# Re-timing the loads and the attention ticks of a fused attention and mixture-of-experts kernel

## The chip, the cores and the metric

The kernel runs on one core of a Trainium2 chip. The metric is the time of one execution on the device, in microseconds (us). The engines are named as in the profile: PE (matrix multiply), DVE (vector), ACT (scalar), POOL and SP; SP and POOL also issue DMA transfers, each from a queue of its own that works in order.

## The reference

Eight sequences of 576 positions pass through a linear attention with 8 heads of 64, and then each whole sequence through one of 8 experts:

```python
# per batch b and head h, for q, k, v of shape (8, 8, 576, 64)
q_s = softmax(q, axis=-1)            # over the 64 channels
k_s = softmax(k, axis=2)             # over the 576 positions
attn = q_s @ (k_s.T @ v)             # (576, 64); heads side by side give x[b]: (576, 512)
# per sequence
logits = x[b].mean(axis=0) @ w_gate  # 8 experts
e = argmax(logits); g = softmax(logits)[e]
out[b] = g * (relu(x[b] @ w1[e]) @ w2[e])   # w1[e]: (512, 1024), w2[e]: (1024, 512)
```

Which expert a sequence takes is known only when its attention is done. With the inputs drawn here the eight sequences take the experts 2, 3, 3, 1, 3, 3, 4, 6: sequences 0, 1, 3, 6 and 7 need an expert that no earlier one had, and sequences 2, 4 and 5 take the one that sequence 1 brought in. All arithmetic of the matrix products is in 16 bit; inputs and weights are 32 bit in memory.

## The kernel before

**Tiles.** A sequence is loaded in two halves, numbered n = 2b and 2b+1, of four heads each. One `load(n)` (L114) is three transfers of 576 KB on SP's queue, q, k and v, each into one of three buffers, so load n+3 waits until n has been read. Per half, `exp_q` and `exp_k` are one ACT instruction each, `cast_v` is one on POOL (or ACT), `scale_q` (L140) is a sum and a reciprocal on DVE and one product, from half 4 on, on POOL. `kv_step` (L156) is 18 small matmuls on PE and four small DVE instructions; `t_step` (L174) transposes 9 blocks on PE into the same two banks of PSUM, and DVE copies them out; `x_step` (L187) multiplies, and DVE (L199) copies the result to `xt` with its row sums.

**Gate.** `gate_step` (L204) multiplies the row sums by `w_gate` on PE, finds the expert on DVE, loads its number into a POOL register and lets POOL issue the transfers of `w1` (L255) and `w2` (L266), 4.2 MB of 32-bit weights, which are cast to 16 bit on the way. There are five slots for weights. Sequence b always uses slot b % 5; if an earlier sequence already holds the expert, the transfers are issued under a condition that is false. `fetch` (L297) then copies each quarter of the weights on DVE from the slot that holds the expert to the sequence's own slot (from the slot to itself when the weights are new). A copy so waits for the transfers.

**Experts.** `moe(b)` (L311) is a generator of 17 units of PE work: 8 of the first product (L320, L325, evicted by ACT in L329), 8 halves of the second (L339), each second one followed by an eviction on ACT (L346) and two output transfers on SP (L348), and the last 64 positions (L354, L359, L361).

**The order of the work** is written out by hand: every engine works its instructions off in the order in which Python emits them. The steps of attention stand in a table of ticks (`at`, L371). A first stretch (L418 to L453) emits sequences 0 and 1; then a loop (L454) takes one unit of `moe(b)` after another, and after each it moves a clock `tick` forward and emits all steps that are due (`run_ticks`). Sequence b's attention stands at ticks 12b to 12b+10, its gate at 12b+10, and its `fetch` at 12(b+1)+6 to +9. In the emission order that follows, sequence 2's attention stands among the units of `moe(0)`, its gate after the first unit of `moe(1)`; sequence 3's attention stands in `moe(1)`, its gate after the first unit of `moe(2)`; and so on. `hold_loads` (L268) puts a tiny transfer on SP that reads from what the fourth of sequence 0's eight transfers of `w1` brings; load 4 and those after it stand behind it on SP's queue.

The lines quoted are those of the kernel before. The whole of it:

Of the kernel before, what the change touches and what calls it, by code (L numbers as in the profile page):

```python
# [10 lines left out]
FP16 = mybir.dt.float16  # L11
# [8 lines left out]
def kernel(  # L20
# [15 lines left out]
    nc = tc.nc  # L36

    B, H, S, Dh = q.shape
# [6 lines left out]
    ND = D // 128  # L45
# [3 lines left out]
    consts = ctx.enter_context(tc.tile_pool(name="consts", bufs=1))  # L49
# [27 lines left out]
    nc.vector.memset(ones_row, 1.0)  # L77
    hist = consts.tile([1, 8], FP32)
    nc.vector.memset(hist, -1.0)
    held = consts.tile([1, 8], FP16)  # L80
    own = consts.tile([1, NS, 8], FP32)
    nc.vector.memset(own, 0.0)
    for n in range(NS):
# [30 lines left out]
    def load(n, names="qkv"):  # L114
        if n >= 2 * B:
            return
        b, i = divmod(n, 2)
        for name in names:
            x = in_pool.tile([128, 2, J * Dh], FP32, name=f"{name}_in")
            nc.sync.dma_start(out=x, in_=pair_src({"q": q, "k": k, "v": v}[name], b, i))  # L120
            ins[n, name] = x.rearrange("p n (j d) -> p n j d", j=J)

    def exp_q(n):
        eq = e_pool.tile([128, J, 2, Dh], FP16, name="eq")
        nc.scalar.activation(out=eq.rearrange("p j n d -> p n j d"), in_=ins.pop((n, "q")), func=AF.Exp)  # L125
        halves[n] = {"eq": eq, "qt": {}, "kv": {}}

    def cast_v(n, on_act=False):
        dst = v_aug[n % NVB][:, :, 1:].rearrange("p j (n d) -> p n j d", n=2)
        if on_act:  # L130
            nc.scalar.copy(dst, ins.pop((n, "v")))
        else:
            nc.gpsimd.tensor_copy(out=dst, in_=ins.pop((n, "v")))  # L133
# [22 lines left out]
    def kv_step(n):  # L156
        ek, va, kps = halves[n]["ek"], v_aug[n % NVB], kv_banks(n)
        for j in range(J):
            for g in range(2):
                r = slice(64 * g, 64 * g + 64)  # L160
                nc.tensor.matmul(  # L161
                    kps[g][:, 0:129], lhsT=ek[r, j], rhs=va[r, j],
                    start=(j == 0), stop=(j == J - 1),
                )
        for g in range(2):
            icv = kv_pool.tile([128, 1], FP32, name="icv")
            nc.vector.reciprocal(out=icv, in_=kps[g][:, 0:1])
            kv = kv_pool.tile([128, 128], FP16, name="kv")
            nc.vector.scalar_tensor_tensor(
                out=kv, in0=kps[g][:, 1:129], scalar=icv, in1=blkmask, op0=ALU.mult, op1=ALU.mult,  # L170
            )
            halves[n]["kv"][g] = kv

    def t_step(n, g):  # L174
        eq = halves[n]["eq"]
        r = slice(64 * g, 64 * g + 64)
        tp = kv_banks(n)[g].bitcast(FP16)[:, 448:448 + S]
        for j in range(J):
            nc.tensor.transpose(out=tp[:, 64 * j:64 * j + 64], in_=eq[r, j], identity=ident[r, r])  # L179
        qt = qt_pool.tile([128, S], FP16, name="qt")  # L180
        if n < 2:
            nc.scalar.copy(qt, tp)
        else:
            nc.vector.tensor_copy(out=qt, in_=tp)  # L184
        halves[n]["qt"][g] = qt

    def x_step(n, g):  # L187
        b, i = divmod(n, 2)
        c = 2 * i + g
        if c == 0:  # L190
            xt = xt_pool.tile([128, ND, S], FP16, name="xt")
            pooled = gat_pool.tile([128, ND], FP32, name="pooled")
            seqs[b] = {"xt": xt, "pooled": pooled}
        xt, pooled = seqs[b]["xt"], seqs[b]["pooled"]
        kvs, qts = halves[n]["kv"], halves[n]["qt"]
        px = bank("x")
        nc.tensor.matmul(px[:, 0:SM], lhsT=kvs[g], rhs=qts[g][:, 0:SM], start=True, stop=True)  # L197
        nc.tensor.matmul(px[:, SM:S], lhsT=kvs[g], rhs=qts[g][:, SM:S], start=True, stop=True)  # L198
        nc.vector.tensor_tensor_reduce(  # L199
            out=xt[:, c, :], in0=px[:, 0:S], in1=ones_f32.to_broadcast([128, S]),  # L200
            scale=1.0, scalar=0.0, op0=ALU.mult, op1=ALU.add, accum_out=pooled[:, c:c + 1],
        )
# [62 lines left out]
            cs = slice(4 * hf, 4 * hf + 4)  # L265
            nc.gpsimd.dma_start(out=w2_all[:, b % NS, cs], in_=w2_src[:, cs], **seqs[b]["kw"])  # L266

    def hold_loads():  # L268

        nc.sync.dma_start(out=held, in_=w1_all[64:65, 0, ND - 1, 0:8])  # L270

    def gate_exp(b):
        ex = gat_pool.tile([1, E], FP32, name="ex")
# [91 lines left out]

    NA = 12
    ticks = {}

    def at(t, fn, *args):  # L371
        ticks.setdefault(t, []).append((fn, args))

    for b in range(B):
        for i in range(2 if b else 0):
            n, t0 = 2 * b + i, NA * b + 5 * i
            at(t0, kv_step, n)
            for g in range(2):
                at(t0 + 1 + g, t_step, n, g)
                at(t0 + 3 + g, x_step, n, g)  # L380
        at(NA * b + 10, gate_step, b)
        late = 0 if b else 5
        at(NA * b + 11 + late, gate_exp, b)
        at(NA * b + 12 + late, gate_split, b)
        at(NA * b + 14 + late, gate_spread, b)
        if b:
            for part in range(2):
                at(NA * (b + 1) + 6 + part, fetch, b, w1_all, part)
                at(NA * (b + 1) + 8 + part, fetch, b, w2_all, part)
    at(15, load_w2, 0)  # L390
    for n in range(4, 2 * B):
        t0 = NA * (n // 2) + 5 * (n % 2)
        x = 3 if n == 4 else 0
        at(t0 - 6 + x, exp_q, n)
        at(t0 - 6 + x, cast_v, n)
        at(t0 - 5 + x, exp_k, n)
        if n + 3 < 2 * B:
            at(t0 - 5 + x, load, n + 3)
        at(t0 - 4 + (x and 2), scale_q, n, nc.gpsimd)
# [15 lines left out]
    load(2)  # L415
    with tc.manual_schedule(engines={ET.PE, ET.DVE, ET.Activation, ET.Pool, ET.SP}):

        exp_q(0)  # L418
        scale_q(0, nc.vector)
        exp_k(0)  # L420
        exp_q(1)
        cast_v(0)
        scale_q(1, nc.gpsimd)
        load(3)
        t_step(0, 0)
        t_step(0, 1)
        kv_step(0)
        exp_k(1)
        cast_v(1, True)
        x_step(0, 0)  # L430
        t_step(1, 0)
        t_step(1, 1)
        x_step(0, 1)
        kv_step(1)
        cast_v(2)
        x_step(1, 0)
        exp_q(2)
        x_step(1, 1)
        exp_k(2)
        run_ticks(11)  # L440
        hold_loads()
        load(4)
        scale_q(2, nc.vector)
        exp_q(3)
        run_ticks(13)
        exp_k(3)
        cast_v(3, True)
        load(5)
        run_ticks(15)
        scale_q(3, nc.vector)  # L450
        tick = NA + 6.0
        run_ticks(tick)
        load(6)  # L453
        for b in range(B):  # L454
            units = 17
            for m, _ in enumerate(moe(b)):
                goal = NA * (b + 2) + 10
                left = units - m
                tick = min(tick + max(0.7, (goal - tick) / left), NA * (b + 3))
                run_ticks(tick)  # L460


# [28 lines left out]
```

The softmax here doesn't subtract the row's maximum and nothing guards it: scores larger than these inputs give would overflow.

## Time and profile before

| | |
|---|---|
| median of 3 runs | 231.9 us (229.86 to 233.02) |
| profiled execution | 232.45 us |
| its span on the core | 230.8 us, 4509 instructions |
| busy: PE, weight loads of PE, DVE, ACT, POOL | 179.8, 94.4, 113.9, 108.6, 68.7 us |
| chain that ended last | PE 52%, DMA 28%, DVE 8% of the span |
| DMA queues | SP 37.76 MB, 50.2% of 16 engines' span; POOL 10.49 MB (as written, 16 bit), 27.9% |

Times in the trace are counted from the start of the span. A busy PE is not PE at its peak: what a matmul costs depends on the clock that PE was granted. A group's idle time is that of its engine just before it, with what ended it. The rates in GB/s count what was written, so a transfer of weights counts with half of what it reads.

### The profile page before, as it was taken

What the parts mean: (1) busy time and instruction counts of PE and PEld (TensorE: products, weight loads), DVE (VectorE), ACT (ScalarE), POOL (GpSimd) and SP (SyncE); (2) the same over time, 40 slices, a digit from 0 to 9 for tenths busy, and PEclk for the clock granted to TensorE, in tenths of its full rate; (3) what the DMA queues carried; (4) which work ended last, traced back from release to release, by engine and by line L of the source; (5) the groups of instructions that cost most, each with busy time, mean ns of one, the idle gap of its engine ahead of it and who ended that gap; (6) DMA issues with size and microseconds to landing.
All of it is one profiled execution on the core that took longest, in us unless ns stands there. A gap on an engine that the chain in (4) does not pass through costs nothing.

```text
span 230.8 us, 4509 instructions
## 1 busy us (share of the span) xinstructions
PE 179.8 (78%) x1608; PEld 94.4 (41%) x1608; DVE 113.9 (49%) x361; ACT 108.6 (47%) x167; POOL 68.7 (30%) x88
## 2 busy tenths in 40 slices
PE   0184369539934999999902999999999998999991
PEld 0152235314412554455401554555445544545540
DVE  0747965514617457765405565775676556120200
ACT  3686005450430755475510473666457423645631
POOL 1232910386202270369000443046126700600000
PEclk9999999855995999999985799999999999999998
DMA  6996799999999883989997164780254995599145
GB/s 207 382 394 250 101 156 289 396 342 275 294 296 363 261 301 84 288 232 256 276 287 272 23 199 151 200 273 4 58 128 74 169 231 119 97 181 268 31 94 112
DMA packets 28807, 48.55 MB, mean 210 GB/s; under 512 B 3184, under 2 KB 10352, under 8 KB 28784
## 3 DMA queue, kind: packets, MB, share of 16 engines
q1 hardware_dynamic: 19472, 37.76, 50.2%
q0 software_dynamic: 8736, 10.49, 27.9%
q8 instruction: 12, 0.20, 0.3%
q10 hardware_dynamic: 576, 0.02, 0.1%
q14 instruction: 11, 0.09, 0.1%
HBM read 61.88 MB, written 9.44 MB: 309 GB/s over the span
## 4 chain that ended last, share of the span: by engine, by line
PE 52%; DMA 28%; DVE 8%; issue 5%; SPq 1%; POOL 1%; POOLq 1%; ACT 1%; DVEq 0%
DMA w_all<-in_moe_w_dram 20%; PE mm L320 19%; PE mm L339 17%; DMA v_in<-in_v_dram 8%; DVE xt L199 3%; PE mm L354 3%; PE x L197 3%; PE kv L161 3%; PE kv L179 3%; PE ht L325 2%; DVE qs L143 2%; DVE w_all L306 1%; SPq L120 1%; PE x L208 1%; POOL w_all L255 1%
## 5 line engine op out<-in xcount | busy, mean ns | idle before, releaser
L320 PE MATMUL mm<-xt,w_all 128*128 128x512 f16 x256 | 67.5, 393 | 0.0
L339 PE MATMUL mm<-w_all,hsb 128*128 128x512 f16 x256 | 63.8, 388 | 0.0
L329 ACT ACTIVATE hsb<-mm 128x512 f16<-128x512 f32 x64 | 37.3, 590 | 37.6 <-PE mm L320 37.6
L146 POOL TENSOR_TENSOR eq<-eq,qsi 128x1152 f16<-128x1152 f16 x13 | 28.8, 2217 | 66.8 <-DVE qsi L145 60.4
L346 ACT ACTIVATE osb<-mm,gate 128x512 f32<-128x512 f32 x32 | 21.9, 686 | 44.2 <-PE mm L339 32.8
L306 DVE COPY w_all<-w_all 128x2048 f16 x28 | 19.1, 682 | 33.2 <-DMA w_all<-in_moe_w_dram 31.1
L199 DVE CUSTOM_DVE_ANT_0 xt<-x,ones_f 128x576 f16<-128x576 f32 x32 | 24.2, 755 | 18.0 <-PE x L198 18.0
L339 PEld LDWEIGHTS <-hsb 128*128 128x128 f16 x256 | 22.3, 99 | 25.2 <-issue 1.6
L197 PE MATMUL x<-qt,kv 128*128 128x512 f16 x32 | 14.0, 439 | 22.9 <-DVE pooled L199 21.4
L320 PEld LDWEIGHTS <-w_all 128*128 128x128 f16 x256 | 20.6, 100 | 20.1 <-issue 4.1
L179 PE MATMUL kv<-ident,eq 64*128 64x64 f16 x270 | 13.7, 200 | 16.7 <-DVE eq L146 9.3
L255 POOL DMA_DIRECT2D w_all<-in_moe_w_dram x36 | 15.1, 426 | 34.2 <-DVE hl L282 17.5
L133 POOL CAST va<-v_in 128x1152 f16<-128x1152 f32 x14 | 16.3, 1163 | 28.1 <-DMA v_in<-in_v_dram 27.9
L143 DVE TENSOR_REDUCE qs<-eq 128x18 f32<-128x1152 f16 x16 | 21.5, 1344 | 5.4 <-ACT eq L125 5.4
L325 PEld LDWEIGHTS <-w_all 128*128 128x128 f16 x256 | 16.6, 100 | 16.0 <-issue 1.6
L184 DVE COPY qt<-kv 128x576 f16<-128x576 f16 x28 | 12.7, 455 | 16.4 <-PE kv L179 16.4
L125 ACT ACTIVATE eq<-q_in 128x1152 f16<-128x1152 f32 x16 | 18.5, 1156 | 4.5 <-DMA q_in<-in_q_dram 4.5
L179 PEld LDWEIGHTS <-eq 64*128 64x128 f16 x288 | 11.1, 102 | 22.9 <-issue 14.8
L137 ACT ACTIVATE ek<-k_in 128x1152 f16<-128x1152 f32 x16 | 18.5, 1154 | 2.2 <-DMA k_in<-in_k_dram 2.2
L325 PE MATMUL ht<-xt,w_all 128*128 128x64 f16 x256 | 18.1, 194 | 0.0
L161 PE MATMUL kv<-va,ek 64*128 64x129 f16 x270 | 12.4, 243 | 4.2 <-POOL va L133 4.2
L359 ACT ACTIVATE osb_t<-mm,gate 128x256 f32<-128x256 f32 x8 | 3.8, 473 | 23.7 <-PE mm L354 23.7
(59 smaller groups left out, 120.8 us busy)
## 6 DMA issues: line engine op xcount, KB each, us to landing
q_in<-in_q_dram SPq DMA_DIRECT2D x16, 576.0 KB, 7.3
k_in<-in_k_dram SPq DMA_DIRECT2D x16, 576.0 KB, 8.9
v_in<-in_v_dram SPq DMA_DIRECT2D x16, 576.0 KB, 10.1
w_all<-in_moe_w_dram POOLq DMA_DIRECT2D x16, 512.0 KB
out_dram<-osb SPq DMA_DIRECT2D x64, 128.0 KB, 4.8
w_all<-in_moe_w_dram POOLq DMA_DIRECT2D x28, 256.0 KB
w_all<-in_moe_w_dram POOLq DMA_DIRECT2D x8, 128.0 KB
out_dram<-osb_t SPq DMA_DIRECT2D x16, 64.0 KB, 2.3
```

The lines of the kernel that those rows point to most:

```text
L143: nc.vector.tensor_reduce(out=qs, in_=eq, op=ALU.add, axis=AX.X)
L146: eng.tensor_tensor(out=eq, in0=eq, in1=qsi.unsqueeze(3).to_broadcast([128, J, 2, Dh]), op=ALU.mult,)
L161: nc.tensor.matmul(kps[g][:, 0:129], lhsT=ek[r, j], rhs=va[r, j], start=(j == 0), stop=(j == J - 1),)
L179: nc.tensor.transpose(out=tp[:, 64 * j:64 * j + 64], in_=eq[r, j], identity=ident[r, r])
L197: nc.tensor.matmul(px[:, 0:SM], lhsT=kvs[g], rhs=qts[g][:, 0:SM], start=True, stop=True)
L199: nc.vector.tensor_tensor_reduce(out=xt[:, c, :], in0=px[:, 0:S], in1=ones_f32.to_broadcast([128, S]), scale=1.0, scalar=0.0, op0=ALU.mult ...
L306: nc.vector.tensor_copy(out=w_all[:, b % NS, cs], in_=w_all[:, ds(seqs[b]["src"], 1), cs].rearrange("p o c f -> p (o c) f"),)
L320: nc.tensor.matmul(phm, lhsT=w1_sb[:, c, fsl], rhs=xt[:, c, 0:SM], start=(c == 0), stop=(c == ND - 1),)
L325: nc.tensor.matmul(pht[:, fc * ST:(fc + 1) * ST], lhsT=w1_sb[:, c, fsl], rhs=xt[:, c, SM:S], start=(fc == 0 and c == 0), stop=(fc == NF - ...
L329: nc.scalar.activation(out=hsb[:, fc, 0:SM], in_=phm, func=AF.Relu)
L339: nc.tensor.matmul(po, lhsT=hsb[:, fc, st * 128:st * 128 + 128], rhs=w2_sb[:, fc, :], start=(fc == 0), stop=(fc == NF - 1),)
L346: nc.scalar.mul(osb, po, gate)
```

## The change

The small transfer `hold_loads` is gone. Loads 4, 5 and 6 are no longer issued in the first stretch and in ticks of `moe(0)`, but all three after the last output transfer of `moe(0)`. The ticks of a sequence's attention begin at a table, `base`: 0, 12, 32, 48, 60, 72, 84, 96 in place of 12b, and each `moe` now has a tick at which it should begin, `starts`: 17, 28, 48, 66, 82, 94, 106, 120. The clock moves so that it reaches the next start when a `moe` ends, and it stands still for the first four units of `moe(1)`. The four `fetch` copies stand 4 to 1 ticks ahead of the start of their own `moe`. `scale_q(3)` is emitted after the last `x_step` of half 2. Four bursts of matmuls whose result nobody reads, `warm`, 55, 10, 4 and 4 of 128 by 128, are put on PE in the first stretch.

In the emission order that follows: `gate_step(1)` comes after the eighth unit of `moe(0)` (before: after the fifth); all of sequence 2's attention stands in `moe(1)`, from its seventh unit on, with the gate after the fourteenth; sequence 3's stands in `moe(2)`, its gate after the tenth unit; sequence 4's begins in `moe(2)` and ends in `moe(3)`, its gate after the fifth unit. From the last units of `moe(3)` on the order is that of before.

```diff
--- before.py
+++ after.py
@@ -77,7 +77,6 @@
     nc.vector.memset(ones_row, 1.0)
     hist = consts.tile([1, 8], FP32)
     nc.vector.memset(hist, -1.0)
-    held = consts.tile([1, 8], FP16)
     own = consts.tile([1, NS, 8], FP32)
     nc.vector.memset(own, 0.0)
     for n in range(NS):
@@ -265,9 +264,11 @@
             cs = slice(4 * hf, 4 * hf + 4)
             nc.gpsimd.dma_start(out=w2_all[:, b % NS, cs], in_=w2_src[:, cs], **seqs[b]["kw"])
 
-    def hold_loads():
-
-        nc.sync.dma_start(out=held, in_=w1_all[64:65, 0, ND - 1, 0:8])
+    def warm(count):
+
+        pw = bank("ht")
+        for n in range(count):
+            nc.tensor.matmul(pw[:, 0:128], lhsT=ident, rhs=blkmask, start=True, stop=True)
 
     def gate_exp(b):
         ex = gat_pool.tile([1, E], FP32, name="ex")
@@ -365,31 +366,33 @@
 
 
 
-    NA = 12
     ticks = {}
+    base = [0, 12, 32] + [12 * b + 12 for b in range(3, B)]
+
+    starts = [17, 28, 48, 66] + [base[b + 1] + 10 for b in range(4, B - 1)] + [base[B - 1] + 24]
 
     def at(t, fn, *args):
         ticks.setdefault(t, []).append((fn, args))
 
     for b in range(B):
         for i in range(2 if b else 0):
-            n, t0 = 2 * b + i, NA * b + 5 * i
+            n, t0 = 2 * b + i, base[b] + 5 * i
             at(t0, kv_step, n)
             for g in range(2):
                 at(t0 + 1 + g, t_step, n, g)
                 at(t0 + 3 + g, x_step, n, g)
-        at(NA * b + 10, gate_step, b)
+        at(base[b] + 10, gate_step, b)
         late = 0 if b else 5
-        at(NA * b + 11 + late, gate_exp, b)
-        at(NA * b + 12 + late, gate_split, b)
-        at(NA * b + 14 + late, gate_spread, b)
+        at(base[b] + 11 + late, gate_exp, b)
+        at(base[b] + 12 + late, gate_split, b)
+        at(base[b] + 14 + late, gate_spread, b)
         if b:
             for part in range(2):
-                at(NA * (b + 1) + 6 + part, fetch, b, w1_all, part)
-                at(NA * (b + 1) + 8 + part, fetch, b, w2_all, part)
+                at(starts[b] - 4 + part, fetch, b, w1_all, part)
+                at(starts[b] - 2 + part, fetch, b, w2_all, part)
     at(15, load_w2, 0)
     for n in range(4, 2 * B):
-        t0 = NA * (n // 2) + 5 * (n % 2)
+        t0 = base[n // 2] + 5 * (n % 2)
         x = 3 if n == 4 else 0
         at(t0 - 6 + x, exp_q, n)
         at(t0 - 6 + x, cast_v, n)
@@ -415,6 +418,7 @@
     load(2)
     with tc.manual_schedule(engines={ET.PE, ET.DVE, ET.Activation, ET.Pool, ET.SP}):
 
+        warm(55)
         exp_q(0)
         scale_q(0, nc.vector)
         exp_k(0)
@@ -424,40 +428,42 @@
         load(3)
         t_step(0, 0)
         t_step(0, 1)
+        warm(10)
         kv_step(0)
         exp_k(1)
         cast_v(1, True)
+        warm(4)
         x_step(0, 0)
         t_step(1, 0)
         t_step(1, 1)
         x_step(0, 1)
         kv_step(1)
         cast_v(2)
+        warm(4)
         x_step(1, 0)
         exp_q(2)
         x_step(1, 1)
         exp_k(2)
         run_ticks(11)
-        hold_loads()
-        load(4)
         scale_q(2, nc.vector)
         exp_q(3)
         run_ticks(13)
         exp_k(3)
         cast_v(3, True)
-        load(5)
-        run_ticks(15)
+        run_ticks(starts[0])
         scale_q(3, nc.vector)
-        tick = NA + 6.0
-        run_ticks(tick)
-        load(6)
+        tick = float(starts[0])
         for b in range(B):
             units = 17
+            goal = starts[b + 1] if b + 1 < B else starts[b]
             for m, _ in enumerate(moe(b)):
-                goal = NA * (b + 2) + 10
-                left = units - m
-                tick = min(tick + max(0.7, (goal - tick) / left), NA * (b + 3))
+                if b == 1 and m < 4:
+                    continue
+                tick += max(0.0, (goal - tick) / (units - m))
                 run_ticks(tick)
+            if b == 0:
+                for n in (4, 5, 6):
+                    load(n)
 
 
 # ---- launch: one core; inputs and outputs as the reference has them ----
```

## The prediction

> **What bounds the kernel now.** I read the page first (the slices and the shares of the chain that ended last), then that chain in order of time, then PE's timeline, then the windows. The chain, cut to its long links:
>
> ```profile
> 25.03 5.19 DMA w_all<-in_moe_w_dram
> ...
> 32.53 11.23 DMA v_in<-in_v_dram
> ...
> 49.46 21.13 DMA w_all<-in_moe_w_dram
> ...
> 104.00 19.84 DMA w_all<-in_moe_w_dram
> ```
>
> Four transfers carry 57 us: the weights of sequences 0, 1 and 3, and half 4's v. What follows the last of them is PE work without a hole: from 130 us on PE is busy in every window. The same on PE's timeline, as idle time in brackets, where PE came to its attention steps too early:
>
> ```profile
> 45.12 1.16 PE L161 MATMUL kv<-va,ek 64*128 64x129 f16 x18 [2.88 <-POOL va L133]
> ...
> 52.41 0.66 PE L179 MATMUL kv<-ident,eq 64*128 64x64 f16 x9 [4.09 <-POOL eq L146]
> ...
> 72.14 0.58 PE L197 MATMUL x<-qt,kv 128*128 128x512 f16 x1 [6.73 <-DVE pooled L199]
> ...
> 125.36 0.59 PE L197 MATMUL x<-qt,kv 128*128 128x512 f16 x1 [9.46 <-DVE pooled L199]
> ```
>
> The last two are named after DVE, but DVE itself stood in `fetch`:
>
> ```profile
> DVE w_all L306 <- DMA w_all<-in_moe_w_dram: 31.1, 6, 9.4
> ```
>
> So sequence 1's weights were asked for at 45.43 (POOL's first issue) and their second half was waited for until 70.7, 25.3 us; sequence 3's were asked for at 100.29 and waited for until 123.94, 23.7 us. Sequences 6 and 7, later and nearly alone, take about 13 us for the same bytes (issue at 197.44, last bytes at about 210.5). The windows say why (columns at the end: PE's clock, DMA share, GB/s as written):
>
> ```profile
> 44.00:48.00 4.00, 2.88 (x24) 1.58 (x24) 1.10 (x5) 2.20 (x3) 2.88 (x5) 0.54 1.04 398
> 50.00:58.00 8.00, 5.59 (x30) 2.48 (x31) 2.74 (x7) 0.55 (x1) 5.56 (x4) 0.50 1.09 274
> ...
> 86.00:92.00 6.00, 6.00 (x58) 2.89 (x57) 3.93 (x13) 2.80 (x4) 0.86 (x1) 1.00 0.35 95
> ...
> 200.00:210.00 10.00, 10.00 (x65) 4.86 (x64) 1.69 (x4) 4.83 (x9) 1.71 (x3) 1.00 1.12 183
> ```
>
> Loads alone move 0.398 MB per us. In 50 to 58 weights and loads share: if the engines take in 0.395 in all and a weight counts double, x + y = 0.274 and x + 2y = 0.395, so weights read 0.24 and loads 0.15. Weights alone read 2 x 0.183 = 0.37. At 86 to 92 the engines are two thirds idle.
>
> **What the Trainium skill says.** "DMA: Bandwidth & Descriptors", section "Issuing engines are not separate DMA queues": transfers from SP, ACT and POOL run on the same 16 engines and interleave. The 274 GB/s above, with the split, agrees; so what SP holds back, POOL's weights gain. "TensorE: Matmul & The Clock Gate", Part 1: PE starts throttled, is released after some 3.4 us of sustained work and throttled again after about as long without. The trace agrees in durations: four L320 took 1.82 us at 32.47 and 1.04 at 34.71, after 4 us of dense work; the clock falls to 0.56 in 68 to 70, 3.5 us after PE stopped. The same part prices a 128-column matmul at 107 ns throttled and 56 ns released; no row of before has that size.
>
> **The change, step by step.** Everything is worked from the profiled execution (230.8 us of span); the median is 1.1 us above that span.
>
> 1. *Warm-up.* 55 x 107 ns = 5.9 us, begun when POOL has made the mask (1.84), ends by 7.8; PE's first step waited until 9.35 anyway. The 10 and 4 and 4 (1.1, 0.4, 0.4 us at most) stand in waits of 1.29, 0.77 and 0.64 us. Hidden; with no cover they would cost up to 7.8 us. Gain: if PE stays released until `gate_step(0)`, `kv_step(1)` falls from 1.14 to 0.70, `t_step(1)` by 0.3 and two `x_step` by 0.2 each: 1.1 us; if not, nothing. I take 1.1: gate at 19.7 instead of 20.76. By 29 us PE has idled enough to be throttled again, I assume.
> 2. *`scale_q(3)` moved.* Its 3.0 us on DVE no longer stand ahead of L199 of half 2, which ended the 3.5 us wait at 30.81. Next late are the weights of sequence 0: landed at 30.24, now 29.1. `moe(0)` starts there, not at 32.47.
> 3. *To gate 1.* Eight units: two throttled (2.0 and 1.6 us), six at 0.99, a throttled `kv_step` 1.1, two `t_step` 0.74, two `x_step` 0.5: 12.0, so the gate at 41.1 (before 39.83, with three units and `kv_step(3)` differently placed). POOL's first issue comes 2.9 us after the gate, as in 97.32 to 100.29: 44.0. Before it was 45.43, since POOL stood in `cast_v(4)` (43.91), which waited for v. It gains 1.4 us.
> 4. *Sequence 1's weights.* Begin to move 1.2 us after issue. `w1`, 2.1 MB at 0.37, 5.7 us, plus 0.8 MB of `moe(0)`'s outputs, 2.1 us: landed at 53.5. SP issues loads 4 to 6 behind the last output, from about 51.5 (before: 31.1). `w2`, 2.1 MB at 0.24 beside them: 8.7 us, landed at 62.3. Before: 70.7. PE ends `moe(0)` at 49.5, waits about 5.5 us for `w1` and two copies (1.4), and reaches the seventh unit of `moe(1)` at 64.
> 5. *Third sequence.* DVE stands in `fetch` until 63.0; behind it in its queue are the sum for half 4 (1.6) and half 4's `kv` scaling, behind those POOL's product (2.2): transposes at 66.8, a wait of PE. Loads at 0.15 until 62, then 0.39, bring half 4's v at about 63.5 and half 5's at 68: both just in time. From 66.8 to gate 2: six half units 5.4, the rest of attention 3.1, DVE order 1.0, throttled clock 0.9: 77.2 (before 75.86). Then gate, `gate_exp`, `gate_split` and two copies with a sum between them, 5.9 us, of which PE covers 2.9: `moe(2)` starts at 83.1. Before: 95.8.
> 6. *Gate 3.* Ten units 9.7, attention 3.8, one sum of 1.6 on DVE ahead of the last L199, clock 0.9: 99.2 (before 97.32). PE is 9 units further, DMA has loads 4 to 11 behind it.
> 7. *Sequence 3's weights.* First issue 102.2. Load 12 (its v stands behind `cast_v(9)`, and that behind POOL's six issues) and two outputs compete; before, two loads did. Start 1.2, `w1` 8.7 at 0.24, the rest of load 12 beside `w2` 5 us, the last 0.9 MB alone 2.3, output 0.7, landing 0.9: 18.8, so 121.0.
> 8. *To the end.* Last copy 0.7, `kv` scaling 1.0, then the order of before from the second unit of `moe(3)`, which took 100.75 us (130.05 to 230.8), plus half 9's steps and the gate 1.5 and a throttled start 1.0: 121.0 + 105 = 226.0.
>
> That is 4.8 us less than 230.8. The copies themselves cost what they did (28 of 0.68 us); removing the small SP transfer (0.78 us) is worth nothing, as SP then only waits for outputs. 231.9 - 4.8 = **227.1 us**, 2.1% faster, on the edge of the 2% that a measurement of this kernel can tell from no change.
>
> **Rivals.**
> *The weights come unhindered* (222 us). PE stays released from 29 on (gate 1 earlier by 2.3) and outputs take nothing from `w1` (2.1): steps 4 to 8 move by 4.4, 226.0 to 221.6. For it: outputs of one sequence spread over 8 us. Against: windows with outputs alone show shares of 0.3 to 0.6 at 64 to 131 GB/s.
> *The third sequence becomes the bound* (236 us). If the three loads take as much from `w2` as before, its first half again comes 25.3 us after the issue, 69.3, its second 71.3, 9 us later than in step 4; DVE's queue then holds up all of sequence 2, and gate 3 and the end move with it: 226 + 9 = 235. It costs nothing until 62.3, the gain is gone at 67, and slower by 2% begins at 71.8. Against it: `w1` is through before the loads start. For: at 44 to 50 loads kept the weights from moving at all.
> *The wait only moves* (231.5 us). Sequence 3's transfer takes 23.7 + 1.5 us as before although one load less competes: 102.2 + 25.2 + 105 = 232.4 of span, 233.5 us, less the 2 by which gate 3 comes earlier if step 5's waits of PE (1.0 for DVE's order, 0.9 for the clock) fall away. No change.
>
> **How the numbers follow.** Forecast 0.43 (its own range 224 to 230), unhindered 0.24, wait moves 0.17, third sequence 0.16. Half of the forecast's range and all of the first rival is faster by over 2%, and the upper part of the third rival's is slower: faster 0.46, same 0.36, slower 0.18. Range 219 to 236: it holds the first rival with the bound of step 1 (nothing to 2.3 us more) and ends where the third sequence's delay is 9 us.
>
> **What would show it.** In the profile after: `moe(0)` from 29; POOL's issues at 44 and 102; SP's load 4 at 51 to 52; PE idle at 50 to 55, again before the transposes of half 4 (66), and some 10 us before 120; `moe(2)` from 83; from 123 on no idle PE. Wrong would make it: weights of sequence 1 landing after 65, PE waiting for v of half 4 or 5, or L199 of sequence 4 not behind a copy.

## The result and the profile after

| | before | after | forecast |
|---|---|---|---|
| median, four runs each on one chip | 232.34 us (229.86 to 233.02) | 246.22 us (242.43 to 248.36) | 227.1 us (219 to 236) |
| ratio after to before, 95% interval | | 1.0508 [1.0377, 1.0639] | |
| span of the profiled execution | 230.8 us | 246.7 us | 226.0 us |

The change makes the kernel 5% slower. The ratio leaves out disturbed executions, among them the profiled one of after (248.36 us, its longest), so its span overstates the loss, and the ledger below also has the experiment e1, which is after without the warm-up (span 245.0 us).

The chain that ended last can be followed back in after only to 88.68 us, so it says nothing of the time ahead of that. From there to 190 us it has a single long transfer, that of sequence 3's weights, 15.8 us later than in before (104.00):

```profile
119.76 17.66 DMA w_all<-in_moe_w_dram
```

The waits of after show that DVE's copies stand longer for the weights (before 31.1 us in 6 waits; columns: sum, number, longest):

```profile
DVE w_all L307 <- DMA w_all<-in_moe_w_dram: 51.7, 8, 10.7
```

PE's timeline of after shows what it does to PE. L321 is the first product, L160, L178 and L196 are `kv_step`, `t_step` and `x_step`, L207 is the gate (in before these lines have other numbers, the gate is L208); the brackets hold PE's idle time and what ended it.

```profile
57.14 1.89 PE L321 MATMUL mm<-xt,w_all 128*128 128x512 f16 x4 [6.65 <-DVE w_all L307]
...
68.47 0.70 PE L160 MATMUL kv<-va,ek 64*128 64x129 f16 x18 [1.90 <-POOL va L132]
...
72.86 0.93 PE L178 MATMUL kv<-ident,eq 64*128 64x64 f16 x18 [2.60 <-POOL eq L145]
...
84.47 0.35 PE L207 MATMUL x<-wg_sb,pooled 128*1 128x8 f32 x8
...
96.23 0.64 PE L178 MATMUL kv<-ident,eq 64*128 64x64 f16 x9 [3.19 <-DVE kv L168]
...
112.76 0.34 PE L207 MATMUL x<-wg_sb,pooled 128*1 128x8 f32 x8 [0.98 <-DVE pooled L198]
...
129.42 0.58 PE L196 MATMUL x<-qt,kv 128*128 128x512 f16 x1 [8.59 <-DVE pooled L198]
...
140.01 0.64 PE L178 MATMUL kv<-ident,eq 64*128 64x64 f16 x9 [5.54 <-DVE kv L168]
```

The two gates in it are those of sequences 2 and 3. The same gates in before, then POOL's first issue for sequence 3 in before and in after:

```profile
75.86 0.35 PE L208 MATMUL x<-wg_sb,pooled 128*1 128x8 f32 x8
...
97.32 0.35 PE L208 MATMUL x<-wg_sb,pooled 128*1 128x8 f32 x8 [0.39 <-DVE pooled L199]
```

```profile
100.29 2.77 POOL L255 DMA_DIRECT2D w_all<-in_moe_w_dram  x4 [1.73 <-DVE hl L282]
```

```profile
116.11 2.77 POOL L254 DMA_DIRECT2D w_all<-in_moe_w_dram  x4 [1.73 <-DVE hl L283]
```

PE's last long wait ended at 125.36 in before and at 140.01 in after. A ledger from one to the next finds the whole loss of span (times in us):

| stretch | before | after | difference | e1 |
|---|---|---|---|---|
| start to gate 2 | 75.86 | 84.47 | +8.6 | 82.78 |
| gate 2 to gate 3 | 21.46 | 28.29 | +6.8 | 27.48 |
| gate 3 to POOL's first issue for sequence 3 | 2.97 | 3.35 | +0.4 | 3.34 |
| issue to the end of PE's last wait for these weights | 25.07 | 23.90 | -1.2 | 24.40 |
| from there to the end of the span | 105.4 | 106.7 | +1.3 | 107.0 |
| sum | 230.8 | 246.7 | +15.9 | 245.0 |

So sequence 3's weights are no slower than before; they are asked for 15.8 us later (13.3 in e1), because two gates are late. The windows of after say what the transfers do meanwhile. The columns are the stretch, its length, the busy time of PE, of PE's weight loads, DVE, ACT and POOL (instructions in brackets), PE's clock, the DMA share and GB/s as written.

```profile
40.00:44.00 4.00, 4.00 (x35) 2.08 (x33) 2.17 (x14) 1.99 (x4) 0.00 (x0) 1.00 0.00 0
50.00:58.00 8.00, 1.35 (x13) 0.49 (x9) 1.54 (x4) 0.70 (x2) 0.00 (x0) 0.83 1.08 236
58.00:66.00 8.00, 8.00 (x50) 3.75 (x49) 0.07 (x1) 3.85 (x6) 0.00 (x0) 0.75 1.12 306
...
120.00:128.00 8.00, 0.84 (x4) 0.29 (x3) 0.96 (x2) 0.69 (x1) 4.86 (x4) 0.72 1.08 253
```

From 40 to 44 nothing moves at all; before, loads moved 385 GB/s in that window:

```profile
40.00:44.00 4.00, 2.25 (x24) 1.23 (x20) 3.27 (x17) 2.65 (x6) 0.09 (x1) 1.00 1.07 385
```

From 50 to 58 the DMA engines are full, and PE works 1.35 us of 8.

### The profile page after: what moved, and what is told of

It is laid out like the page before. It is cut to its first block, busy times and chain, and to the rows that moved or that the text cites. A ratio compares the mean times of both kernels' runs of the same rounds, so it can differ in the third digit from the quotient of the medians.

```text
span 246.7 us, 4631 instructions
## 1 busy us (share of the span) xinstructions
PE 193.7 (79%) x1681; PEld 103.2 (42%) x1681; DVE 118.0 (48%) x361; ACT 109.3 (44%) x167; POOL 68.8 (28%) x88
## 4 chain that ended last, share of the span: by engine, by line
PE 33%; DMA 12%; DVE 12%; issue 4%; POOLq 1%; POOL 0%; ACT 0%; DVEq 0%
PE mm L321 14%; DMA w_all<-in_moe_w_dram 12%; PE mm L340 10%; DVE w_all L307 4%; DVE xt L198 3%; DVE qs L142 3%; PE kv L178 2%; PE ht L326 2%; PE kv L160 1%; PE mm L355 1%; PE x L196 1%; PE x L207 1%; DVE kv L168 1%; POOLq L254 0%; DVE qt L183 0%
## 5 line engine op out<-in xcount | busy, mean ns | idle before, releaser
L321 PE MATMUL mm<-xt,w_all 128*128 128x512 f16 x256 | 73.1, 415 | 9.9 <-DVE w_all L307 9.0
L330 ACT ACTIVATE hsb<-mm 128x512 f16<-128x512 f32 x64 | 37.8, 593 | 61.9 <-PE mm L321 61.9
L307 DVE COPY w_all<-w_all 128x2048 f16 x28 | 22.4, 801 | 52.9 <-DMA w_all<-in_moe_w_dram 51.7
L145 POOL TENSOR_TENSOR eq<-eq,qsi 128x1152 f16<-128x1152 f16 x13 | 28.3, 2177 | 58.3 <-DVE qsi L144 54.9
L347 ACT ACTIVATE osb<-mm,gate 128x512 f32<-128x512 f32 x32 | 21.9, 685 | 41.5 <-PE mm L340 29.7
L321 PEld LDWEIGHTS <-w_all 128*128 128x128 f16 x256 | 21.4, 103 | 33.4 <-DVE w_all L307 10.7
L178 PE MATMUL kv<-ident,eq 64*128 64x64 f16 x270 | 14.0, 204 | 16.3 <-DVE kv L168 12.2
L132 POOL CAST va<-v_in 128x1152 f16<-128x1152 f32 x14 | 16.9, 1210 | 31.0 <-DMA v_in<-in_v_dram 30.8
L326 PEld LDWEIGHTS <-w_all 128*128 128x128 f16 x256 | 17.3, 103 | 17.5 <-issue 4.3
L196 PE MATMUL x<-qt,kv 128*128 128x512 f16 x32 | 14.4, 449 | 12.4 <-DVE pooled L198 12.0
L178 PEld LDWEIGHTS <-eq 64*128 64x128 f16 x288 | 11.7, 104 | 21.8 <-issue 14.1
L326 PE MATMUL ht<-xt,w_all 128*128 128x64 f16 x256 | 18.9, 199 | 0.0
L160 PE MATMUL kv<-va,ek 64*128 64x129 f16 x270 | 12.8, 248 | 2.5 <-POOL va L132 2.5
L160 PEld LDWEIGHTS <-ek 64*128 64x128 f16 x288 | 10.9, 111 | 6.3 <-issue 4.0
```

The lines of the kernel that those rows point to most:

```text
L145: eng.tensor_tensor(out=eq, in0=eq, in1=qsi.unsqueeze(3).to_broadcast([128, J, 2, Dh]), op=ALU.mult,)
L160: nc.tensor.matmul(kps[g][:, 0:129], lhsT=ek[r, j], rhs=va[r, j], start=(j == 0), stop=(j == J - 1),)
L307: nc.vector.tensor_copy(out=w_all[:, b % NS, cs], in_=w_all[:, ds(seqs[b]["src"], 1), cs].rearrange("p o c f -> p (o c) f"),)
L321: nc.tensor.matmul(phm, lhsT=w1_sb[:, c, fsl], rhs=xt[:, c, 0:SM], start=(c == 0), stop=(c == ND - 1),)
L326: nc.tensor.matmul(pht[:, fc * ST:(fc + 1) * ST], lhsT=w1_sb[:, c, fsl], rhs=xt[:, c, SM:S], start=(fc == 0 and c == 0), stop=(fc == NF - ...
L330: nc.scalar.activation(out=hsb[:, fc, 0:SM], in_=phm, func=AF.Relu)
```

## The experiments

Times are medians, each ratio is to the kernel before on the same chip, with its 95% interval. My theory after the result was that the loss is the lead: how far a gate stands ahead of the mixture that needs its weights. Rivals were the warm-up, the late loads by themselves, and the copies placed just ahead of their mixture.

**e1, no warm-up.** After, without the four calls of `warm`.

> The changed kernel without its 73 warm-up matmuls. Theory: the warm-up bought nothing, since the 18 matmuls of half 0 at 11.13 us ran throttled (1.16 us) in spite of it and gate 0 came only 0.4 us sooner; so the time stays that of the changed kernel, 243 to 248 us. Rival (the warm-up keeps PE fast through the first sequence): 2 to 4 us slower than the changed kernel.

Measured: 245.51 us, 1.0584 [1.0489, 1.0679]. Gates 2 and 3 at 82.78 and 110.26, waits of 8.98 and 6.22 us for sequence 3's weights in place of 8.59 and 5.54. Neither a cost nor a gain of the warm-up can be told from these runs, and the waits of after are not of its one long execution. In after's own timeline it is seen why it brings so little there: the transposes of half 0 run released (0.58 us, before 0.90), and 1.8 us later `kv_step(0)` is throttled (1.16 us; 0.70 for the same 18 matmuls where it runs released, at 68.47).

```profile
9.31 0.58 PE L178 MATMUL kv<-ident,eq 64*128 64x64 f16 x18 [1.56 <-DVE eq L145]
...
11.13 1.16 PE L160 MATMUL kv<-va,ek 64*128 64x129 f16 x18 [0.57 <-POOL va L132]
```

**e2, loads early.** After, with `hold_loads` and loads 4, 5 and 6 where before has them:

```diff
         run_ticks(11)
+        hold_loads()
+        load(4)
...
+        load(5)
...
+        load(6)
...
-            if b == 0:
-                for n in (4, 5, 6):
-                    load(n)
```

> The changed kernel, but loads 4, 5 and 6 are issued where the kernel before has them, behind the small transfer that waits for sequence 0's weights. Theory A (the loads are late, and with them all of the third sequence): gate 2 moves from 84.5 to about 80 us or sooner, the end by as much or more, 238 to 241 us. Theory B (the third sequence stands behind the weight copies in DVE's queue, whenever its loads come): sequence 1's weights share with the loads and land no sooner than at 66 us, gate 2 stays within 2 us of 84.5, and the time is 243 to 247 us.

Measured: 244.01 us, 1.0555 [1.0459, 1.0651]. Now the loads slow the weights, and PE's wait grows instead of going away. DVE's and PE's timeline of e2:

```profile
59.32 1.42 DVE L312 COPY w_all<-w_all 128x2048 f16 x2 [13.24 <-DMA w_all<-in_moe_w_dram]
```

```profile
60.07 1.89 PE L326 MATMUL mm<-xt,w_all 128*128 128x512 f16 x4 [9.21 <-DVE w_all L312]
```

Half 4's v is there (POOL casts it at 49.99, in after at 67.07), but its steps stand in the order behind the seventh unit of `moe(1)`. Gate 2 comes at 81.87, 2.6 us sooner than in after and between what the two theories gave; by the ratio the time gains nothing. Late loads alone are not the cause.

**e3 and e4, loads kept off the weights.** The kernel before, with loads 12 and 13 (e3), or 7, 8 and 9 (e4), issued later, behind the weights of sequence 3 or of sequence 1. This is the thought of the change, to hold loads back for the sake of weights, done alone and with the order of PE, DVE, ACT and POOL untouched (shown is e3; e4's table is `{4: 30, 5: 31, 6: 33}`):

```diff
-            at(t0 - 5 + x, load, n + 3)
+            late_load = {9: 58, 10: 59}
+            at(late_load.get(n, t0 - 5 + x), load, n + 3)
```

> The kernel before, with loads 12 and 13 issued only after the first two units of moe(3), so that sequence 3's weights do not share with them. Theory (what is worth holding back are loads that nobody waits for while weights are in flight): the weights land 14 to 16 us after their first issue in place of 23.7, PE's wait of 9.5 us before 125 us shrinks to 0 to 2, and the kernel takes 222 to 226 us. Rival (the transfers take as long, or the wait reappears later on the deferred loads): 229 to 234 us.

> The kernel before, with loads 7, 8 and 9 issued in the last third of moe(0), so that sequence 1's weights share with loads 5 and 6 only. Theory: the second half of the weights lands at 62 to 65 us in place of 70.7, PE's wait of 6.7 us shrinks to 0 to 2, and the end comes 4 to 6 us sooner, 226 to 229 us. Rival (sequence 3's attention now waits for its loads): v of half 6 or 7 ends a wait of PE in moe(1), and the time is 231 us or more.

Measured: e3 221.99 us, 0.9579 [0.9507, 0.9651]; e4 225.21 us, 0.9743 [0.9655, 0.9832]. In e3 sequence 3's weights take 16.3 us from the first issue (100.44) to the copy of their second half, not 23.7, and PE's 9.46 us wait is 2.07 (DVE's and PE's timeline):

```profile
116.70 0.69 DVE L306 COPY w_all<-w_all 128x2048 f16 x1 [3.10 <-DMA w_all<-in_moe_w_dram]
```

```profile
118.12 0.38 PE L197 MATMUL x<-qt,kv 128*128 128x512 f16 x1 [2.07 <-DVE pooled L199]
```

In e4 sequence 1's second half is copied 19.1 us after the issue at 45.06 (before 25.3), and gate 2 comes at 68.38 instead of 75.86. The loss does not come from holding loads back as such: where the order of attention stays, that is a gain of 4.2% and of 2.6%.

**f1, the lead of sequence 3, the fourth.** After, with one entry of `base` changed (48 to 42), so that gate 3 is emitted after four units of `moe(2)` rather than ten; all of sequence 3's attention and loads 9 and 10 move forward with it:

```diff
-    base = [0, 12, 32] + [12 * b + 12 for b in range(3, B)]
+    base = [0, 12, 32, 42] + [12 * b + 12 for b in range(4, B)]
```

> The changed kernel with sequence 3's attention at ticks 42 to 52 in place of 48 to 58, so that its gate stands 13 units of PE ahead of moe(3) in place of 7. Theory (the shortened lead of gate over moe exposes the transfer of new weights): POOL's first issue for sequence 3 moves from 116 us to about 109 or sooner, PE's waits for these weights (8.6 and 5.5 us) lose half or more, and the time is 236 to 241 us. Rival (the loads or the vector engine hold sequence 3's attention back anyway): the issue stays at 114 us or later and the time at 244 to 248 us.

Measured: 236.43 us, 1.016 [1.0086, 1.0235]: 9.8 us less than after by the medians, 3.5% of before (some 8 us) by the ratios, and no longer 2% above before. PE's timeline of f1:

```profile
99.62 0.34 PE L207 MATMUL x<-wg_sb,pooled 128*1 128x8 f32 x8
...
118.27 0.59 PE L196 MATMUL x<-qt,kv 128*128 128x512 f16 x1 [3.83 <-DVE pooled L198]
...
128.19 0.64 PE L178 MATMUL kv<-ident,eq 64*128 64x64 f16 x9 [5.42 <-DVE kv L168]
```

The gate is 13.1 us earlier than in after, the end 12.3 by the spans (against e1 10.6 and 10.6); PE's first wait is less than half as long, the second as long, and both come over 11 us sooner.

**f2, load 12 behind the weights.** After, with load 12 at tick 66 (`at(66 if n == 9 else t0 - 5 + x, load, n + 3)`).

> The changed kernel with load 12 issued after the first unit of moe(3), so that no load shares with sequence 3's weights. Theory: the weights are complete some 4 us sooner after their first issue (21.4 us to the first half of w2 in the changed kernel), and the time falls by as much, to 240 to 243 us. Rival (it is outputs and the transfer itself, not the one load): less than 1.5 us.

Measured: 237.74 us, 1.0215 [1.0125, 1.0305]: 8.5 us less than after by the medians, 2.9% of before (some 7 us) by the ratios, more than was expected. The weights take 16.4 us from issue (111.62) to the second half's copy, in place of 21.4 in after:

```profile
137.52 0.69 DVE L307 COPY w_all<-w_all 128x2048 f16 x1 [8.15 <-DMA w_all<-in_moe_w_dram]
```

The issue itself comes 4.5 us sooner than in after, which isn't the edit's doing: e1 and e2, without it, issue at 113.60 and 111.91, and then need 21.9 and 21.2 us. Against e2, which issues at the same time, f2's span is 7.4 us shorter (234.8 for 242.2): 4.8 us lie between the issue and the copy, 2.3 behind the copy. Why the rest behind the copy is shorter too was not taken apart.

**g2, the lead of sequence 2, the third, alone.** e2 with `base[2] = 24` and `starts[1] = 34`, the values of the order before.

> The changed kernel with early loads, and with sequence 2's attention back at ticks 24 to 34 and moe(1) back at tick 34, so that this attention stands ahead of the copies of sequence 1's weights in DVE's queue. Theory (what early loads alone could not give, since the attention stood behind the waiting copies): gate 2 comes at 76 to 79 us in place of 81.9 with early loads alone, gate 3 at 102 to 105 in place of 108.6, and the time is 237 to 240 us. Rival (PE has that work to do anyway, so only its place moves): gate 3 within 2 us of 108.6 and 242 to 245 us.

Measured: 244.27 us, 1.0563 [1.0507, 1.0619]. My theory fell in this form: gate 2 comes at 79.72, 2.2 us sooner than in e2, and gate 3 at 110.41, 1.8 us later than there. In g2 PE has worked off five units of `moe(1)` at gate 2, in after fourteen; gate 3 stays tied to the tenth unit of `moe(2)`, so the other nine come between the two gates. The work only changed its place, as the rival said.

**g3, copies without POOL beside them.** After, with half 6's product on DVE in place of POOL. In after two copies of `w2` for sequence 2 took 3.79 us instead of 1.4, while POOL had a product and a cast (DVE's, then POOL's timeline of after):

```profile
90.98 0.65 DVE L307 COPY w_all<-w_all 128x2048 f16 x1
...
91.93 3.79 DVE L307 COPY w_all<-w_all 128x2048 f16 x2
```

```profile
91.24 2.37 POOL L145 TENSOR_TENSOR eq<-eq,qsi 128x1152 f16<-128x1152 f16 x1 [0.38 <-DVE qsi L144]
93.56 1.62 POOL L132 CAST va<-v_in 128x1152 f16<-128x1152 f32 x1
```

> The changed kernel with half 6's product on DVE, so that POOL has no product beside the copies for sequence 2. Theory (DVE's copies are slowed by POOL's work on the same memory at the same time): the two copies of w2, 2.24 and 1.53 us in the changed kernel, take 0.7 us each, or one of them up to 1.5 beside a POOL cast. Rival (they wait for the skipped transfers of the gate on POOL): they stay at 3.8 us together. The time hardly changes, 243 to 247 us, since DVE does the product instead.

Measured: 243.74 us, one run, so the time tells little. In g3 the two copies take 1.42 together:

```profile
90.71 1.42 DVE L307 COPY w_all<-w_all 128x2048 f16 x2
```

So the copies are slowed by POOL's work beside them, and not by the skipped transfers, which g3 has too (83.96 to 86.22). In g3 DVE spends 1.99 us on the product itself.

**g4 and h1, both leads.** g4 is e2 with `base = [0, 12, 24, 36, 60, ...]` and `starts[1] = 34`: gates 2 and 3 stand where before has them in the clock of ticks.

> As lead of sequence 2, and sequence 3's attention back at ticks 36 to 46 too: what is left of the change are the warm-up, the ticks from sequence 4 on and scale_q(3). Theory (the loss is the shortened leads of gate over moe): within 2% of the kernel before, 229 to 235 us. Rival (copies close to their moe, or the ticks of sequences 4 and 5, cost by themselves): 237 us or more.

Measured: 244.41 us, 1.0594 [1.0523, 1.0665], though gate 3 came at 94.94. The edit had brought a new wait. The last copy of sequence 2's weights, at tick 47, now stood behind gate 3 (tick 46), and POOL had issued sequence 3's transfers before it. DVE's and PE's timeline of g4:

```profile
111.97 0.69 DVE L312 COPY w_all<-w_all 128x2048 f16 x1 [14.90 <-DMA w_all<-in_moe_w_dram]
```

```profile
113.20 0.16 PE L297 MATMUL x<-hl,ones_row 1*128 1x2 f16 x1 [14.85 <-DVE hl L289]
```

The weights that this copy reads, sequence 1's, had long been there. It reads a slot whose number stands in a register, and what fits the wait is that it has to wait for every transfer into the weights' buffer that is under way, here another sequence's. h1 is g4 with sequence 2's four copies two ticks sooner, ahead of gate 3:

```diff
-                at(starts[b] - 4 + part, fetch, b, w1_all, part)
-                at(starts[b] - 2 + part, fetch, b, w2_all, part)
+                at(starts[b] - (6 if b == 2 else 4) + part, fetch, b, w1_all, part)
+                at(starts[b] - (4 if b == 2 else 2) + part, fetch, b, w2_all, part)
```

> The kernel after with the loads 4, 5, 6 where the kernel before has them, the bases of the second to fourth sequence 12, 24, 36 as before (the first mixture's ticks from 17 to 34), and the copies of the third sequence's weights two ticks sooner (42 to 45), so that they stand ahead of gate 3's transfers. Theory (the whole loss is the lead of the attention over the mixtures, and the loads of the weights that hang on it): 229 to 236, with gate 3 below 98 and no wait over 3 us of a copy for the fourth sequence's weights. Rival (something else in the change costs too, such as the copies just ahead of their mixture or the ticks from the fifth sequence on): 240 or more although gate 3 is below 98.

Measured: 227.14 us, 0.9744 [0.9667, 0.982], below the 229 to 236 that the theory gave. PE's timeline of h1, then DVE's:

```profile
94.99 0.34 PE L208 MATMUL x<-wg_sb,pooled 128*1 128x8 f32 x8
...
117.51 0.50 PE L197 MATMUL x<-qt,kv 128*128 128x512 f16 x1 [3.83 <-DVE pooled L199]
```

```profile
119.03 0.69 DVE L312 COPY w_all<-w_all 128x2048 f16 x1 [1.57 <-DMA w_all<-in_moe_w_dram]
```

With the loads and leads of before, everything else in the change (warm-up, `scale_q(3)` moved, copies just ahead of their mixture, the ticks from the fifth sequence on) costs nothing in sum: h1 is 7.6% of before faster than after by the ratios. Of the parts of h1's edit, the early loads (e2) and sequence 2's lead on top of them (g2) gave nothing that the ratios can tell; sequence 3's lead alone (f1) gave 3.5%. With it gate 3 came at 99.62, and with both leads at 94.99; how the rest of the gain divides between sequence 2's lead, the loads and the copies was not taken apart. The wait of PE that is left, 3.83 us, is behind two copies that took 2.39 and 1.27 us beside POOL's work. The 4.9 us by which h1's span is shorter than before's (225.9 for 230.8) lie ahead of the copy at 119.03: the issue is 1.9 us sooner (98.41 for 100.29), and from it to the copy it takes 20.6 us in place of 23.7; behind the copy both take 106.9. Why the transfer is shorter is open.

**h2, f1 and f2 together.**

> The kernel after with its fourth sequence's base at 42 and load 12 at tick 66, the two single edits that gave 236.4 and 237.7 from 246.2. If they take away different parts of the lateness of the fourth sequence's weights (issue at 116.1 and transfer of 21.4 us), they add: 227 to 230, second half of w2 copied at 118 to 122. If what stands behind the weights is by then something else (the first three sequences' attention, gate 3 at 99.6), the second edit adds less than 4: 232.5 or more.

Measured: 238.92 us, 1.0276 [1.0204, 1.0348]: they do not add. The rival said so. Issue at 105.19, the first half of `w2` copied at 126.44, 21.2 us later, about as in after: with the gate earlier, load 11 (issued 106.2 to 111.2) now falls behind it and beside the weights. In f2, where load 11 was issued from 103.6 to 106.0, ahead of the weights, and the same eight outputs ran beside them, it took 16.4 us; so load 11 seems to take the room that load 12 left.

**f3, the best version.** Before, with e3's and e4's table in one: `late_load = {4: 30, 5: 31, 6: 33, 9: 58, 10: 59}`.

> The kernel before with loads 7, 8, 9 and 12, 13 deferred, both edits that were run singly. Theory (two separate waits, of 6.7 and 9.5 us, each removed once): the gains of 7.0 and 10.2 us add up but for the starts in between, 215 to 218 us. Rival (the gain of the one is given back in the other, since sequence 3's gate then comes 7 us sooner and its weights meet other loads): 220 to 223 us.

Measured: 215.9 us, 0.9206 [0.9118, 0.9295]; the two gains, 10.2 and 7.0 us by the medians, add to 17.0 (by the ratios 4.2% and 2.6%, together 7.9%). It beats both kernels: sequence 3's weights take 14.7 us from the issue at 92.42 to the second half's copy (DVE's timeline of f3), and after 52 us PE has no wait of 1 us or more.

```profile
107.10 0.69 DVE L306 COPY w_all<-w_all 128x2048 f16 x1 [1.54 <-DMA w_all<-in_moe_w_dram]
```

The pages' slices of PE's clock show what comes with it, first f3, then after: from the tenth slice on, the clock falls with the long waits of PE (in f3 at its 5.51 us wait before 51.63), so that PE pays for them once more.

```profile
PEclk9999999997599999999999999999999999999999
```

```profile
PEclk9855569995985997699956689999999999999999
```

The slices ahead of that can't be compared. In f3 they read full, but `kv_step(2)` at 21.01 took 1.16 us there, as at 20.66 in after, where the slice reads 5.

**f4 and g5, more of the same.** f4 is f3 with `scale_q(3)` behind half 2 as in the change, and `cast_v(4)` one tick later.

> As defer both, and also the one piece of the change that looked right: scale_q(3) behind the last x_step of half 2; and cast_v(4) behind gate 1 on POOL, so that the weights of sequence 1 are asked for before POOL waits for v. Theory: moe(0) starts at 30.3 in place of 32.5 us, POOL's first issue for sequence 1 comes at 43 in place of 45 us, and the kernel is 1 to 2 us faster than with the deferred loads alone. Rival (PE waits for half 4's v at 44 us anyway, and weights asked for sooner only meet more loads): no difference, within 0.7 us.

Measured: 215.75 us, 0.9255 [0.9175, 0.9336], no difference from f3, as the rival said: PE waits 6.51 us for half 4's v until 49.34, where f3 had waits of 2.31 and 5.51 us. g5 is f3 with load 6 at tick 27 as well, and half 4's product on DVE.

> The kernel before with loads 7 to 9 and 12, 13 deferred, and load 6 too (behind moe(0)'s first outputs), with half 4's product on DVE. Theory (every load that is not needed before the weights costs the weights its share): sequence 1's weights are complete at 58 to 60 us in place of 63, and the time is 210 to 213 us. Rival (half 6 then comes late, ACT or PE waits for its q or v, or PE's own work is the bound by now): 215 us or more.

Measured: 219.41 us, 0.948 [0.9386, 0.9574], slower than f3: sequence 1's second half is copied later (65.54, f3 63.76), and PE waits 10.36 us until 67.69, behind that copy. DVE's, then PE's timeline of g5:

```profile
65.54 1.43 DVE L306 COPY w_all<-w_all 128x2048 f16 x1 [8.56 <-DMA w_all<-in_moe_w_dram]
```

```profile
67.69 0.59 PE L197 MATMUL x<-qt,kv 128*128 128x512 f16 x1 [10.36 <-DVE pooled L199]
```

Both held loads now fall beside these weights, asked for from 44.52 on: load 6 was issued from 51.41 (f3: 36.15, ahead of the weights) and load 7 from 54.37 (f3: 61.29, just before they were there). Load 7 has the same tick in both; PE, without f3's 5.51 us wait, simply got there sooner. Holding back by a place in the order has this end: the load comes whenever the order gets there.

## Why the prediction was wrong

The sign was wrong. The nearest text on record is the rival "the third sequence becomes the bound": late weights of sequence 1 hold up DVE's queue, and with it sequence 2, gate 3 and the end. That is how it began, but the lateness of these weights is only 4.4 us of the 20.7 by which the span of after missed the forecast; the larger part came in links that this rival does not have. By the prediction's own steps:

1. *Warm-up.* Gate 0 at 20.37, forecast 19.7: the clock was not kept. Nothing that can be told at the end (e1).
2. *`scale_q(3)`.* Right: `moe(0)` starts at 28.20, waits for weights as foreseen, and goes on at 30.05 (forecast 29.1).
3. *To gate 1.* Right within a microsecond: 41.93 and POOL's first issue at 44.83, forecast 41.1 and 44.0.
4. *Sequence 1's weights.* The first step that failed, as a size. `w1` was to land at 53.5 and was copied at 56.39; `w2` was to land at 62.3 and was copied at 66.70. The addends of this step give 53.0, not 53.5, so the miss is no slip of the sum. The argument that "`w1` is through before the loads start" did not hold: load 4 was issued from 52.77 to 55.34, before `w1` was in. Outputs and load 4 together took more of `w1`'s time than the 2.1 us that I gave the outputs, and I gave `w2` 0.24 MB per us beside the loads; from 58 to 66 it was, by the same split, x + y = 0.306 and x + 2y = 0.395, so 2y = 0.18, an estimate. Together 4.4 us. DVE's timeline of after:

```profile
56.39 1.42 DVE L307 COPY w_all<-w_all 128x2048 f16 x2 [10.68 <-DMA w_all<-in_moe_w_dram]
...
66.70 2.26 DVE L307 COPY w_all<-w_all 128x2048 f16 x2 [8.63 <-DMA w_all<-in_moe_w_dram]
```

5. *Third sequence.* Transposes at 72.86, forecast 66.8; gate 2 at 84.47, forecast 77.2. The transposes are late by step 4's 4.4 and 1.7 more, behind the sum and the scaling on DVE and the product on POOL, which all waited for the copies; 0.9 of the 1.7 is the copies' own time, 2.26 us for two in place of 1.4. 1.2 more came by the gate. Two signs that were named as wrong appeared here: weights of sequence 1 after 65, and PE waiting for v of half 4 (cast at 67.07, forecast 63.5; 1.90 us at 68.47).
6. *Gate 3.* The second step that failed. 99.2 was forecast from 22.0 us after gate 2; it took 28.3. The 6.3 us are links on DVE and POOL that I did not price (they overlap, so their times are no sum): six transfers of the gate for sequence 2, skipped, still kept POOL 2.3 us (87.31 to 89.58) and the first copy 1.32; two copies took 3.79 us in place of 1.4; behind them DVE's `kv` scaling left PE 3.19 us idle; and PE, throttled by these pauses, needed 1.82, 1.82 and 1.43 us for what was counted at 1.04 (96.87 to 103.4). Of these only the two copies were tested singly (g3). e1 and e2 show the same stretch at 27.5 and 26.7 us.
7. *Sequence 3's weights.* First issue at 116.11, forecast 102.2. Then 22.7 us to the second copy of the second half (138.80), forecast 18.8: +3.9. The forecast had load 12 in it, but too cheaply: without load 12 beside them the same stretch takes 17.7 us (f2, 111.62 to 129.32). The figure of "about 13 us" for weights nearly alone was too low beside the 25.3 and 23.7, which run to the copy: to the copy (213.37) that transfer took 15.9 us.
8. *To the end.* 107.9 us from 138.80, forecast 105: +2.9.

The errors add up: 7.3 (gate 2) + 6.3 + 0.4 (gate to issue) + 3.9 + 2.9 = 20.8, against 246.7 - 226.0 = 20.7. The steps that failed are above all 4, 6 and 7: the time of sequence 1's weights, of the stretch from gate 2 to gate 3, and of sequence 3's weights, all three too short.

Behind these sizes stands a choice that I did not examine. I counted that gate 3 now comes after the tenth unit of `moe(2)`, where it came after the first, so that seven units and their share of attention, some 10 us, are all that is left to hide a transfer of about 20 us. But I let the forecast of gate 3 rest on gate 2 and so took every saving upstream for one at the end. f1 shows the price of that one placement, 3.5% or some 8 us; h1 shows that with both placements undone, and loads and copies to match, nothing of the loss is left. The third rival, that the wait only moves, named the right place (sequence 3's weights) and missed that the issue itself moves. Taking loads from beside sequence 1's weights was worth 7 us in e4, which holds back loads 7 to 9. The change holds back loads 4 to 6, which sequence 2's attention needs first, and issues them while these weights still move: from issue to the second half's copy it takes 21.9 us (44.83 to 66.70), 25.3 before, 19.1 in e4.

The Trainium skill, "DMA: Bandwidth & Descriptors", "Issuing engines are not separate DMA queues", was borne out and carried the right half: what SP holds back POOL gains (e3, e4). What stays open: why f2 is also faster behind the copy, and why the weights of sequence 3 come sooner in h1 than before.

## What to carry to other kernels

Where data decide what is loaded, the decision's lead over its use is the number to protect: count in the emission order the work that stands between a gate's issue and the first reader of its weights, and compare it with the transfer's own time beside what else is due. Hold back a load that competes with an urgent transfer, but only if its consumer stands after that transfer anyway; move the load alone, leave the order of the compute, and look where the new order puts it, since a load held to a later place can fall beside the very weights that it was to spare (g5). And a copy through a register's slot is best put ahead of the next issue into that buffer (g4, h1).

## What the runs showed of the hardware

- *A copy on DVE waits for POOL's instruction.* The Trainium skill, "SBUF — State Buffer", section "SBUF: two separate sides", says that DVE's operations in a 2-port mode and GpSimd's share a pair of ports by an exclusive lock, held for a whole instruction. That this copy runs in such a mode no run shows, but the trace of after agrees: in the 3.79 us of two copies, the first ends (94.16) 0.55 us after POOL's product (93.61), the second (95.72) 0.54 us after POOL's cast (95.18), as if each ran once POOL was done (0.69 is its time alone). In g3, with no work of POOL beside them, both together take 1.42.
- *A skipped transfer isn't free.* Under a false condition each of POOL's issues still stands about 0.45 us apart (0.41 of it named as a wait for the buffer's transfers); six take 2.3 us (87.31 to 89.58 in after), and a copy that reads the buffer waited for them, 1.32 us until 88.81.
- *The warm-up's release varies.* 55 matmuls of 128 columns took 5.87 us in after, 107 ns each and throttled throughout, and 4.69 us in h1; with the 107 and 56 ns of the Trainium skill, "TensorE: Matmul & The Clock Gate", Part 1, an estimate for h1 is a release after 3.4 us (3.4 / 0.107 + 1.3 / 0.056 = 55), which is what that page names. In after it came later than the burst, and was lost again within 2 us (transposes of 0.58 us at 9.31, `kv_step` of 1.16 at 11.13).
- *The record of the clock can read full where the durations don't.* From 20 to 30 us it reads 1.00 in before and 0.50 in after, though `kv_step(2)` takes 1.16 us in both (21.05 and 20.66), and 0.70 where PE runs released. So a mean clock of a kernel with the warm-up can't be set against one without.
